# Output projection of the last segment: its first 384 columns under the last attention unit's combination

## The chip, the cores and the metric

The kernel runs on one core of a Trainium2 chip. TensorE (PE) does the matrix products, VectorE (DVE) and ScalarE (ACT) the element-wise work and all reading of PSUM, GpSimd (POOL) element-wise work in SBUF; SyncE (SP), ACT and POOL also issue DMA transfers. The metric is the device time of one execution in microseconds. Every engine takes its instructions in the order in which the program lists them and waits at each for the semaphores that it names.

## The reference

One transformer block on a 2048 x 576 input, float32:

```python
mod = (_silu(c) @ w_mod).reshape(c.shape[0], 6, 1, -1)
sa, ca, ga, sb, cb, gb = (mod[:, 0], ..., mod[:, 5])
h = _layernorm(x) * (1 + ca) + sa
x = x + ga * _A_ref(h, wq, wk, wv, wo, beta)     # attention
h = _layernorm(x) * (1 + cb) + sb
return x + gb * _B_ref(h, w_gate, w_up, w_down)  # (silu(h @ w_gate) * (h @ w_up)) @ w_down
```

The attention has 32 heads of 18 columns and works on 4 segments of 512 rows. In each segment it mixes causal softmax attention within the segment with a linear attention over a memory of the segments before it, and multiplies the 576 columns by `wo`. The FFN has 4608 inner columns.

## The kernel before

Every float32 product is made of three products of float32r parts: an operand x is split into `hi`, a cast of it, and `lo = x - hi`, and hi\*hi, hi\*lo and lo\*hi are summed in PSUM.

The program has three stages. The first makes q, k, v of the segments. The second runs 32 units (segment s, group q of 4 heads, u = 8 s + q). The third is the FFN, in 18 pairs of blocks of 256 inner columns, done by a scheme with seven products instead of eight (`step`, `prod`).

The second stage's order is written out by hand: `ORDER` (L60 to L94) has one line of tokens for each unit, and `act` turns each token into the instructions of one small step. What matters here: `a` makes a unit's scores in banks of the tags `s1` (3 buffers) and `s2` (3 buffers); `V0123` makes P\*V of a unit into a bank `av` of the tag `x` (2 buffers); `E` copies it to SBUF (`avs`, ACT, L726); `c` transposes it (`px`, PE, L735); `d` divides by the row sums and adds the result into the unit's 72 columns of `o` (DVE, L743 to L752). `>` moves a token to the next unit; `y` and a number are steps that make inputs of the FFN, `M0` to `M3` and `X` a half of an output projection.

The output projection of segment s takes `o` (4 groups i of 128 rows, 576 columns) through these steps: `wo_r` transposes columns 0 to 511 of a group into one bank `pto` (four transposes, L789); `wo_s` casts it to `hh` (ACT, L795); `wo_t` makes `hl` from `pto` and `hh` (DVE, L799); `wo_z` and `wo_z2` do the same with columns 512 to 575 of all four groups (`ptr`, `or`; L772, L778, L779); `wo_m` makes 14 products for each group and half h of the 576 output columns into a bank `pw` (L815): for segment 3 first the eight with `hh`, then four with `hl`, then two with `or`; `wo_x` adds `pw` to the input rows `xr` (DVE, L820), and after h = 1 a DMA stores them (L822).

For segments 0 to 2 these steps stand among later units. Segment 3 has no later units: its steps are written out behind `ORDER`, after the pools of the second stage are closed, with a PSUM pool of their own (`pst`, tags `x` with 4 and `w` with 2 buffers). In between stand, on the SP queue, the loads of the FFN's first weights (`O`, L1290: pair 0's two halves) and of four of its inputs (`y`, L1277 and L1278), and within the loop over the eight (i, h) the first weights are prepared: `sum_o` (L1312) makes sums of weight blocks, `prep_w` casts (`wh`, ACT, L1321) and subtracts (`wl`, DVE, L1322), `y_here` makes three more inputs (L1197, L1199), `store_o` writes the sums to DRAM for later (`oD`, L1296), `store_r` does so with the cast row remainders (`rD`, L1315). `O` has two buffers, so that the next pair's load (L1290) into a buffer waits for the store of `oD` that reads it.

Of the kernel before, what the change touches and what calls it, by code (L numbers as in the profile page):

```python
# [7 lines left out]
F32 = mybir.dt.float32  # L8
# [3 lines left out]
ALU = mybir.AluOpType  # L12
PSUM = bass.MemoryType.PSUM
DRAM = bass.MemoryType.DRAM

P = 128
S = 2048
# [5 lines left out]
L = 512  # L23
# [29 lines left out]
WC = 4  # L53
# [40 lines left out]
)  # L94
LNA = 1
# [1 line left out]
S1B, S2B, XB = 3, 3, 2  # L97
# [8 lines left out]
def block(ctx: ExitStack, tc: tile.TileContext, x, wqk, wv, wo, beta, wgu, wd, c, w_mod, wm01, out):  # L106
    nc = tc.nc
    def pool(stk, name, bufs=1, **kw):
        return stk.enter_context(tc.tile_pool(name=name, bufs=bufs, reuse_waits="tile", **kw))
# [16 lines left out]
    ident = cst.tile([P, P], F32, tag="ident", name="ident")  # L126
# [159 lines left out]
    p2, p2q, p2r, p7 = ExitStack(), ExitStack(), ExitStack(), ExitStack()  # L286
# [43 lines left out]
    with ExitStack() as p1:  # L330
        raw = pool(p1, "raw1", 2)
        x1 = pool(p1, "x1")
        w1 = pool(p1, "w1")
        wk = pool(p1, "wk1", 2)
        ps = pool(p1, "ps1", 2, space=PSUM)
# [84 lines left out]
        with ExitStack() as p0:  # L420
# [39 lines left out]
            for b in range(3):  # L460
                n = P if b < 2 else 64
# [202 lines left out]
    vp = pool(p2, "vp", 2)  # L664
    pp_ = pool(p2, "pp")
    wk = pool(p2, "wk2", 2)
    ps = pool(p2, "ps2", 2, space=PSUM)

    def load_unit(u):
        if u < NU:  # L670
            load_stack(u, u % NB)
# [82 lines left out]
    ot, vq = {}, {}  # L754

    def load_v(s, j):
        if j == 0:
            vq[s] = vp.tile([P, 4, VC], F32, tag="vq", name=f"vq{s}")
        nc.sync.dma_start(vq[s][:, j, :], vD[s][:, j, :])
# [7 lines left out]
    oT, orr, pto = {}, {}, {}  # L767

    def wo_z(s):
        pt = ps.tile([P, 4, P], F32, tag="x", name="ptr", bufs=XB if s < 3 else 4)  # L770
        for i in range(4):
            nc.tensor.transpose(pt[:64, i, :], ot[s][:, i, 512:576], ident)  # L772
        pto[s] = pt
# [7 lines left out]
    def load_xr(s, i):  # L781
        xr = o3.tile([P, D], F32, tag="xr", name="xr") if s < 3 or i in (0, 3) else xp.tile([P, D], F32, tag="xs", name="xr")
        nc.sync.dma_start(xr, x[s][:, i, :])
        return xr

    def wo_r(s, i):
        pt = ps.tile([P, 4, P], F32, tag="x", name="pto", bufs=XB if s < 3 else 4)
        for kt in range(4):
            nc.tensor.transpose(pt[:, kt, :], ot[s][:, i, 128 * kt:128 * kt + 128], ident)  # L789
        pto[s, i] = pt  # L790
        oh, ol = [hvp.tile([P, L], F32R, tag=f"{n}{i % 2}", name=n).rearrange("p (a b) -> p a b", b=P) for n in ("hh", "hl")]
        oT[s, i] = (oh, ol, load_xr(s, i) if s < 3 else xr3[i])

    def wo_s(s, i):
        nc.scalar.copy(oT[s, i][0], pto[s, i])  # L795

    def wo_t(s, i):
        oh, ol, _ = oT[s, i]
# [2 lines left out]
    wps = {}  # L801

    def wo_m(s, i, h, c):
        oh, ol, _ = oT[s, i]
        sl = slice(288 * h, 288 * h + 288)
        if c == 0:
            wps[0] = ps.tile([P, L], F32, tag="x" if s < 3 else "w", name="pw", bufs=XB if s < 3 else 2)
        ops = []
        for k in range(4):
            ops += [(oh[:, k], woh[:, k, sl]), (oh[:, k], wol[:, k, sl]), (ol[:, k], woh[:, k, sl])]  # L810
        if s == 3:
            ops = [ops[n] for n in (0, 1, 3, 4, 6, 7, 9, 10, 2, 5, 8, 11)]
        ops += [(orr[s][:, i], woh[:, 4, sl]), (orr[s][:, i], wol[:, 4, sl])]
        for n in range(14 * c // WC, 14 * (c + 1) // WC):
            nc.tensor.matmul(wps[0][:, :288], lhsT=ops[n][0], rhs=ops[n][1], start=(n == 0), stop=(n == 13))  # L815

    def wo_x(s, i, h):
        xr = oT[s, i][2]
        sl = slice(288 * h, 288 * h + 288)
        nc.vector.tensor_tensor(xr[:, sl], wps[0][:, :288], xr[:, sl], op=ALU.add)  # L820
        if h == 1:
            (nc.scalar if (s, i) == (2, 3) else nc.sync).dma_start(xD[s][:, i, :], xr)  # L822

# [536 lines left out]
    T, SG, AC, AP = {}, {}, {}, {}  # L1360
# [158 lines left out]
    with tc.manual_schedule():  # L1519
# [7 lines left out]
        def step_a(u):  # L1527
            if u not in flows:
                ma, mb = [], []
                flows[u] = (chain(*[p2_step(u, j, ma) for j in range(4)]), p1_seq(u + 2, mb), ma, mb)  # L1530
            scores(*flows[u])

        def act(tok, u):
            nonlocal w3, o3, opl_, woh, wol
            if tok[0] in "<>":
                act(tok[1:], u + (1 if tok[0] == ">" else -1))
            elif tok == "a":
                step_a(u)
            elif tok == "U":
                load_unit(u + 3)  # L1540
            elif tok[0] == "v":
                load_v(u // 8 + 1, int(tok[1]))
            elif tok == "SA":
                stage_a()
            elif tok == "SB":
                stage_b()
            elif tok[0] == "y":
                parts[int(tok[1:])]()
            elif tok == "O":
                p2q.close()  # L1550
                w3 = pool(p2r, "w3", side="right")
                o3 = pool(p2r, "o3", 2, side="right")
                opl_ = pool(p2, "op2", side="right")
                woh = w3.tile([P, 5, D], F32R, tag="woh", name="woh")
                wol = w3.tile([P, 5, D], F32R, tag="wol", name="wol")
                ot[0] = opl_.tile([P, 4, D], F32, tag="o0", name="o0")
            else:
                event(tok, u)
# [3 lines left out]
                act(tok, u)  # L1562
        p2.close()
        mid.close()
        ps = pool(p2r, "pst", 2, space=PSUM)
        xp = pool(p4, "xp", 2)
        yp = pool(p4, "yp")
        y = yp.tile([P, 7, 5, L], F32R, tag="y", name="y")
# [4 lines left out]
        xr3 = {i: load_xr(3, i) for i in range(3)}  # L1573
# [9 lines left out]
        xr3[3] = load_xr(3, 3)  # L1583
        load_y(0, 5)
        load_y(0, 3)
        wo_r(3, 0)
        wo_z(3)
        wo_r(3, 1)
        wo_s(3, 0)
        wo_t(3, 0)  # L1590
        wo_z2(3)
        wo_s(3, 1)
        wo_t(3, 1)
        gw = iter(MP[:PF])
        for i in range(4):
            for h in range(2):
                for c in range(WC):
                    n = 8 * i + 4 * h + c
# [28 lines left out]
        ps = pool(p4, "ps4", 1, space=PSUM)  # L1627
# [6 lines left out]
        n, nw = 0, PF  # L1634
# [200 lines left out]
```

## Time and profile before

| | us |
|---|---|
| runs, median of 3 | 1833.85 (1831.41 to 1834.4) |
| profiled execution, its own time | 1828.63 |
| span of the profiled execution | 1826.8 |
| mean granted TensorE clock in it | 0.999 of full |
| the 512 products on L815, segments 0 to 3: first and last start | 310.1, 563.5 |
| first product of the FFN (L1357) | 563.60 |

The runs are of the kernel alone; the profiled execution is one more, and its span is what lies between the first and the last event of its trace. In a row of the order of time stand the start, the time from the start of the first to the end of the last instruction of the row, the engine, the line, the operation, what it writes and reads, and in brackets the idle time of the engine before it with what ended it. In a row of windows stand the window, its length, the busy time of PE, of PE's weight loads, DVE, ACT and POOL with the number of instructions, the granted clock, the busy share of the DMA engines and GB/s. In a row of the waits of the SP queue stand the waiting line, what it waited for, the sum, the number of waits and the longest one.

### The profile page before, as it was taken

How to read it: one execution, taken by the hardware profiler on the slowest of the kernel's cores; microseconds unless marked ns; L12 is line 12 of the kernel's file. 1: busy time of each engine (PE TensorE's matmuls, PEld its weight loads, DVE VectorE, ACT ScalarE, POOL GpSimd, SP SyncE). 2: the span in 40 equal slices, each digit the busy share in tenths (PEclk: the TensorE clock that was granted, in tenths of full speed). 3: DMA queues.
4: the chain of work that ended last, by engine and by line, in shares of the span. 5: the costliest groups of instructions: out<-in, count | busy, mean ns of one | idle time of the engine just before them, and what ended most of it. 6: DMA issues, size and time to landing. Idle time of an engine off the chain costs nothing.

```text
span 1826.8 us, 31122 instructions
## 1 busy us (share of the span) xinstructions
PE 1802.9 (99%) x11061; PEld 1514.3 (83%) x11061; DVE 1490.4 (82%) x3309; ACT 953.8 (52%) x2137; POOL 492.6 (27%) x702
## 2 busy tenths in 40 slices
PE   8999999999999999999999999999999999999999
PEld 5888766766668888888888888888888888888888
DVE  7566588998968888888888898668888888888886
ACT  6443577777875444544454444434544544544541
POOL 2000146555660554465354544100000000000000
PEclk9999999999999999999999999999999999999999
DMA  8677765567659545544653454594334324323331
GB/s 297 227 237 274 242 179 162 150 197 208 186 175 315 175 163 182 191 154 164 200 173 128 151 170 133 168 303 151 96 96 128 101 85 129 107 79 129 106 103 52
DMA packets 178562, 304.49 MB, mean 167 GB/s; under 512 B 25304, under 2 KB 108184, under 8 KB 176616
## 3 DMA queue, kind: packets, MB, share of 16 engines
q1 hardware_dynamic: 151032, 248.66, 43.0%
q10 hardware_dynamic: 27376, 53.86, 8.4%
q8 instruction: 87, 1.43, 0.3%
q14 instruction: 67, 0.55, 0.1%
HBM read 188.42 MB, written 113.33 MB: 165 GB/s over the span
## 4 chain that ended last, share of the span: by engine, by line
PE 92%; DMA 3%; DVE 3%; issue 1%; ACT 1%; SPq 0%; ACTq 0%; DVEq 0%
PE A L1357 24%; PE pd L1485 13%; PE C L1357 12%; PE pd L1466 10%; PE B L1357 6%; PE pp L553 4%; PE av L714 4%; PE pw L815 3%; PE s L691 3%; PE s L204 3%; PE pv L582 2%; PE pp L839 2%; DMA y<-yD 1%; DMA qs<-mr 1%; PE pw L892 1%; PE pn L951 1%
## 5 line engine op out<-in xcount | busy, mean ns | idle before, releaser
L1357 PE MATMUL A<-y,wh 128*128 128x512 f32 x1152 | 406.1, 393 | 1.3 <-ACT B L1403 0.9
L1357 PEld LDWEIGHTS A<-y,wh 128*128 128x128 f32 x1152 | 216.6, 188 | 46.0 <-ACT B L1403 2.2
L1322 DVE TENSOR_TENSOR wl<-O,wh 128x256 fp32r<-128x256 f32 x504 | 249.4, 500 | 2.1 <-ACT wh L1321 1.6
L219 DVE CUSTOM_DVE_ANT_0 junk<-s,tri 128x384 bf16<-128x384 f32 (+3 forms) x512 | 221.6, 486 | 30.0 <-PE s L204 13.2
L1357 PE MATMUL A<-y,wl 128*128 128x512 f32 x576 | 226.8, 394 | 0.0
L1471 DVE TENSOR_TENSOR acc<-acc,pd 128x576 f32<-128x576 f32 x216 | 162.2, 752 | 58.9 <-PE pd L1466 51.2
L1357 PE MATMUL C<-y,wh 128*128 128x512 f32 x576 | 203.0, 393 | 0.5 <-DVE cu L1380 0.5
L1321 ACT CAST wh<-O 128x256 fp32r<-128x256 f32 x504 | 197.5, 405 | 0.7 <-DMA yD<-st 0.7
L697 ACT ACTIVATE Pt<-s 128x512 f32<-128x512 f32 (+2 forms) x384 | 179.4, 528 | 31.6 <-PE s L691 18.1
L1485 PE MATMUL pd<-dh,ah 128*128 128x288 f32 x640 | 189.1, 295 | 0.5 <-DVE x L1489 0.5
L1495 DVE TENSOR_TENSOR acc<-acc,pd 128x576 f32<-128x576 f32 x156 | 116.9, 750 | 89.1 <-PE pd L1485 88.3
L1485 PE MATMUL pd<-dh,al 128*128 128x288 f32 x640 | 189.1, 295 | 0.0
L1312 POOL TENSOR_TENSOR O<-O 128x384 f32<-128x384 f32 x132 | 150.4, 1153 | 143.3 <-DMA O<-in_wgu_dram 55.5
L1485 PE MATMUL pd<-dl,ah 128*128 128x288 f32 x640 | 188.8, 295 | 0.0
L1426 ACT CAST ah<-sg 128x512 fp32r<-128x512 f32 x192 | 119.1, 620 | 78.4 <-DVE sg L1381 71.9
L1427 DVE TENSOR_TENSOR al<-sg,ah 128x512 fp32r<-128x512 f32 x192 | 136.2, 709 | 10.3 <-ACT ah L1426 10.2
L1466 PE MATMUL pd<-dh,ah 128*128 128x288 f32 x448 | 133.0, 297 | 0.0
L1466 PE MATMUL pd<-dh,al 128*128 128x288 f32 x448 | 132.5, 296 | 0.0
L1466 PE MATMUL pd<-dl,ah 128*128 128x288 f32 x448 | 132.3, 295 | 0.0
L1485 PEld LDWEIGHTS pd<-dh,ah 128*128 128x128 f32 x640 | 120.8, 189 | 6.8 <-DVE x L1489 0.8
L1485 PEld LDWEIGHTS pd<-dl,ah 128*128 128x128 f32 x640 | 120.5, 188 | 7.1
L1357 PEld LDWEIGHTS C<-y,wh 128*128 128x128 f32 x576 | 108.3, 188 | 21.5 <-DVE cu L1380 1.3
(410 smaller groups left out, 4337.7 us busy)
## 6 DMA issues: line engine op xcount, KB each, us to landing
O<-in_wgu_dram SPq DMA_DIRECT2D x36, 768.0 KB
O<-oD SPq DMA_DIRECT2D x36, 512.0 KB
oD<-O ACTq DMA_DIRECT2D x34, 512.0 KB
ks<-kD SPq DMA_DIRECT2D x64, 216.0 KB
qs<-qD SPq DMA_DIRECT2D x64, 216.0 KB
O<-in_wgu_dram SPq DMA_DIRECT2D x36, 384.0 KB
rD<-wr ACTq DMA_DIRECT2D x36, 336.0 KB
wr<-rD SPq DMA_DIRECT2D x35, 336.0 KB
```

The costliest lines, as they stand in the source:

```text
L219: nc.vector.tensor_tensor_reduce(junk[:, :n], bank[:, n * o:n * o + n], tri[:, L - n:], 1.0, -3e38, op0=ALU.add, op1=ALU.max, accum_out=mx ...
L697: nc.scalar.activation(pt[:, hs[0]:hs[-1] + 1:2, :n], bank[:, :n * per].rearrange("p (a b) -> p a b", a=per), AF.Exp, scale=SCALE)
L1312: eng.tensor_tensor(o[:, d], o[:, a], o[:, b], op=op)
L1321: nc.scalar.copy(wh, o)
L1322: later.append(lambda: nc.vector.tensor_tensor(wl, o, f32(wh), op=ALU.subtract))
L1357: nc.tensor.matmul(bank, lhsT=a, rhs=b, start=(first and n == 0), stop=(n == 6), skip_group_check=not first)
L1426: nc.scalar.copy(ah, src)
L1427: later.append(lambda: nc.vector.tensor_tensor(al, src, f32(ah), op=ALU.subtract))
L1466: nc.tensor.matmul(pd[:, i, :288], lhsT=a[:, tk], rhs=w, start=(k == 0), stop=(k == 2))
L1471: nc.vector.tensor_tensor(o, o, pd[:, :, :288], op=ALU.add)
L1485: nc.tensor.matmul(pd[:, i, :288], lhsT=a[:, tk], rhs=w, start=(k == 0), stop=(k == 5))
L1495: nc.vector.tensor_tensor(o, o, pd[:, :, :288], op=ALU.add)
```

## The change

In the last line of `ORDER`, tokens are put in around the last unit's `c` and `d`. `t0` and `t1` transpose columns 0 to 383 of the groups 0 and 1 of segment 3, `s0` and `s1` cast them, and `w0` and `w1` make the first six products (k = 0 to 2, with `hh`) of group 0 for both halves. Behind `ORDER` only what depends on columns 384 to 511 is left of these steps (`wo_k3`, a cast of 128 columns, products from the seventh on); `wo_t` still makes `hl` of all 512 columns at once. The pool `pst` is gone: the second stage's PSUM pool stays open until the projection is done, `pto` uses the banks of tag `s1`, `pw` those of `s2`, and `ptr` those of `x`.

```diff
-    "... >M2 >M3 y130 >X >V0123 >E y126 >c >d y131",
+    "... >M2 >M3 y130 >X >V0123 >E t0 t1 s0 y126 >c w0 w1 s1 >d y131",
...
-    ps = pool(p2, "ps2", 2, space=PSUM)
+    ps = pool(p2r, "ps2", 2, space=PSUM)
...
-        pt = ps.tile([P, 4, P], F32, tag="x", name="ptr", bufs=XB if s < 3 else 4)
+        pt = ps.tile([P, 4, P], F32, tag="x", name="ptr", bufs=XB)
...
-    def wo_r(s, i):
-        pt = ps.tile([P, 4, P], F32, tag="x", name="pto", bufs=XB if s < 3 else 4)
-        for kt in range(4):
+    def wo_r(s, i, early=False):
+        if s < 3:
+            pt = ps.tile([P, 4, P], F32, tag="x", name="pto", bufs=XB)
+        else:
+            pt = ps.tile([P, 4, P], F32, tag="s1", name="pto", bufs=S1B)
+        for kt in range(3 if early else 4):
             nc.tensor.transpose(pt[:, kt, :], ot[s][:, i, 128 * kt:128 * kt + 128], ident)
...
+    def wo_k3(i):
+        nc.tensor.transpose(pto[3, i][:, 3, :], ot[3][:, i, 384:512], ident)
+
+    def wo_s(s, i, k=slice(0, 4)):
+        nc.scalar.copy(oT[s, i][0][:, k], pto[s, i][:, k])
...
-        if c == 0:
-            wps[0] = ps.tile([P, L], F32, tag="x" if s < 3 else "w", name="pw", bufs=XB if s < 3 else 2)
+        if s < 3 and c == 0:
+            wps[0] = ps.tile([P, L], F32, tag="x", name="pw", bufs=XB)
+        elif s == 3 and (i, h) not in wps:
+            wps[i, h] = ps.tile([P, L], F32, tag="s2", name="pw", bufs=S2B)
...
-        for n in range(14 * c // WC, 14 * (c + 1) // WC):
-            nc.tensor.matmul(wps[0][:, :288], lhsT=ops[n][0], rhs=ops[n][1], start=(n == 0), stop=(n == 13))
+        n0 = 6 if s == 3 and i == 0 else 0
+        for n in range(6) if c < 0 else range(n0 + (14 - n0) * c // WC, n0 + (14 - n0) * (c + 1) // WC):
+            nc.tensor.matmul(pw[:, :288], lhsT=ops[n][0], rhs=ops[n][1], start=(n == 0), stop=(n == 13))
...
+            elif tok in ("t0", "t1"):
+                wo_r(3, int(tok[1]), True)
+            elif tok in ("s0", "s1"):
+                wo_s(3, int(tok[1]), slice(0, 3))
+            elif tok in ("w0", "w1"):
+                wo_m(3, 0, int(tok[1]), -1)
...
-        ps = pool(p2r, "pst", 2, space=PSUM)
...
-        wo_r(3, 0)
+        wo_k3(0)
         wo_z(3)
-        wo_r(3, 1)
-        wo_s(3, 0)
+        wo_k3(1)
+        wo_s(3, 0, slice(3, 4))
         wo_t(3, 0)
         wo_z2(3)
-        wo_s(3, 1)
+        wo_s(3, 1, slice(3, 4))
         wo_t(3, 1)
```

On PE, before, behind the last unit's P\*V (`av`), to the first products with `hl` (`o_6638` is segment 3's `o`):

```order
L714 MATMUL av<-Pt,vq_6127 32x128 x2
L735 MATMUL px<-ident,avs 128x128 [waits DVE_49,Activation_49]
L735 MATMUL px<-ident,avs 128x128 x3
L789 MATMUL pto<-ident,o_6638 128x128 [waits DVE_49,PE_49]
L789 MATMUL pto<-ident,o_6638 128x128 x2
L789 MATMUL pto<-ident,o_6638 128x128 [waits DVE_49,Pool_49]
L772 MATMUL ptr<-ident,o_6638 64x128 x4
L789 MATMUL pto<-ident,o_6638 128x128 x4
L815 MATMUL pw<-woh,hh 128x288 [waits Activation_49]
```

The same place with the change (of the products only those that wait are shown):

```order
L714 MATMUL av<-Pt,vq_6127 32x128 x2
L792 MATMUL pto<-ident,o_6638 128x128 x6
L735 MATMUL px<-ident,avs 128x128 [waits DVE_49,Activation_49]
L735 MATMUL px<-ident,avs 128x128 x3
L826 MATMUL pw<-woh,hh 128x288 [waits Activation_49]
...
L798 MATMUL pto<-ident,o_6638 128x128 [waits DVE_49,Pool_49]
L772 MATMUL ptr<-ident,o_6638 64x128 [waits PE_49]
L772 MATMUL ptr<-ident,o_6638 64x128 x3
L798 MATMUL pto<-ident,o_6638 128x128 [waits Activation_49]
L826 MATMUL pw<-woh,hh 128x288 [waits Activation_49]
...
L826 MATMUL pw<-woh,hl 128x288 [waits DVE_49]
...
L826 MATMUL pw<-woh,or 128x288 [waits DVE_49]
```

Six of the eight transposes stand ahead of `px` and wait for nothing; twelve products stand between `px` and the transpose of columns 384 to 511, which is the one that still waits for DVE's add into `o`. The same stretch on ACT, before:

```order
L726 COPY avs<-av 128x512 [waits PE_49,Activation_49]
L795 CAST hh<-pto 128x512 [waits PE_49]
L778 CAST or<-ptr 64x512 [waits PE_49]
L795 CAST hh<-pto 128x512 [waits PE_49,Activation_49]
```

and with the change:

```order
L726 COPY avs<-av 128x512 [waits PE_49,Activation_49]
L801 CAST hh<-pto 128x384 [waits PE_49]
L801 CAST hh<-pto 128x384 [waits PE_49,Activation_49]
L801 CAST hh<-pto 128x128 [waits PE_49]
L778 CAST or<-ptr 64x512 [waits PE_49]
L801 CAST hh<-pto 128x128 [waits PE_49]
```

Each cast of `hh` is split in two, and the first parts stand right behind `avs`. On DVE, POOL and SP the instructions and their order are the same.

More of the change, by code (lines that the diff above doesn't have):

```diff
@@ L791, in wo_r @@
         oh, ol = [hvp.tile([P, L], F32R, tag=f"{n}{i % 2}", name=n).rearrange("p (a b) -> p a b", b=P) for n in ("hh", "hl")]
-        oT[s, i] = (oh, ol, load_xr(s, i) if s < 3 else xr3[i])
-    def wo_s(s, i):
-        nc.scalar.copy(oT[s, i][0], pto[s, i])
+        oT[s, i] = (oh, ol, load_xr(s, i) if s < 3 else None)
+    def wo_k3(i):
+        nc.tensor.transpose(pto[3, i][:, 3, :], ot[3][:, i, 384:512], ident)
+    def wo_s(s, i, k=slice(0, 4)):
+        nc.scalar.copy(oT[s, i][0][:, k], pto[s, i][:, k])
     def wo_t(s, i):
@@ L805, in wo_m @@
         sl = slice(288 * h, 288 * h + 288)
-        if c == 0:
-            wps[0] = ps.tile([P, L], F32, tag="x" if s < 3 else "w", name="pw", bufs=XB if s < 3 else 2)
+        if s < 3 and c == 0:
+            wps[0] = ps.tile([P, L], F32, tag="x", name="pw", bufs=XB)
+        elif s == 3 and (i, h) not in wps:
+            wps[i, h] = ps.tile([P, L], F32, tag="s2", name="pw", bufs=S2B)
+        pw = wps[0] if s < 3 else wps[i, h]
         ops = []
@@ L812, in wo_m @@
             ops = [ops[n] for n in (0, 1, 3, 4, 6, 7, 9, 10, 2, 5, 8, 11)]
-        ops += [(orr[s][:, i], woh[:, 4, sl]), (orr[s][:, i], wol[:, 4, sl])]
-        for n in range(14 * c // WC, 14 * (c + 1) // WC):
-            nc.tensor.matmul(wps[0][:, :288], lhsT=ops[n][0], rhs=ops[n][1], start=(n == 0), stop=(n == 13))
+        if c == WC - 1:
+            ops += [(orr[s][:, i], woh[:, 4, sl]), (orr[s][:, i], wol[:, 4, sl])]
+        n0 = 6 if s == 3 and i == 0 else 0
+        for n in range(6) if c < 0 else range(n0 + (14 - n0) * c // WC, n0 + (14 - n0) * (c + 1) // WC):
+            nc.tensor.matmul(pw[:, :288], lhsT=ops[n][0], rhs=ops[n][1], start=(n == 0), stop=(n == 13))
     def wo_x(s, i, h):
-        xr = oT[s, i][2]
+        xr = oT[s, i][2] if s < 3 else xr3[i]
+        pw = wps[0] if s < 3 else wps.pop((i, h))
         sl = slice(288 * h, 288 * h + 288)
-        nc.vector.tensor_tensor(xr[:, sl], wps[0][:, :288], xr[:, sl], op=ALU.add)
+        nc.vector.tensor_tensor(xr[:, sl], pw[:, :288], xr[:, sl], op=ALU.add)
         if h == 1:
```

2 rows, old and new, of the table ORDER are left out of this document.

## The prediction

> **What bounds the kernel now.** I read the page first, then the order of time around the place of the change, engine by engine, then the clock, and at last the DMA queue behind it.
>
> ```profile
> span 1826.8 us, 31122 instructions
> PE 1802.9 (99%) x11061; PEld 1514.3 (83%) x11061; DVE 1490.4 (82%) x3309; ACT 953.8 (52%) x2137; POOL 492.6 (27%) x702
> PE 92%; DMA 3%; DVE 3%; issue 1%; ACT 1%; SPq 0%; ACTq 0%; DVEq 0%
> ```
>
> TensorE is busy 99% of the span and makes 92% of the chain of waits: what shortens the kernel is a hole in PE, or a stretch in which PE runs below its rate. Both lie where the last attention unit hands over to the output projection of segment 3. PE in order of time there:
>
> ```profile
> 540.22 0.62 PE L714 MATMUL av<-Pt,vq 128*32 128x256 f32 x12
> 541.60 0.66 PE L735 MATMUL px<-ident,avs 128*128 128x128 f32 x4 [0.76 <-ACT avs L726]
> 544.13 0.52 PE L789 MATMUL pto<-ident,o 128*128 128x128 f32 x3 [1.88 <-DVE tmp L751]
> 545.16 0.30 PE L789 MATMUL pto<-ident,o 128*128 128x128 f32 x1 [0.51 <-DVE o L752]
> 545.30 0.61 PE L772 MATMUL ptr<-ident,o 128*64 128x128 f32 x4
> 545.74 1.02 PE L789 MATMUL pto<-ident,o 128*128 128x128 f32 x4
> 546.41 0.59 PE L815 MATMUL pw<-woh,hh 128*128 128x288 f32 x1
> ...
> 549.60 0.29 PE L815 MATMUL pw<-woh,hh 128*128 128x288 f32 x1
> ...
> 551.47 0.60 PE L789 MATMUL pto<-ident,o 128*128 128x128 f32 x4
> ```
>
> The brackets are holes: 0.76, 1.88 and 0.51 us. The first 14 products take 549.60 - 546.41 = 3.19 us, the next 14 only 551.47 - 549.60 = 1.87 us (0.134 us each). The granted clock (the third number from the right in these windows) says why:
>
> ```profile
> 545.60:545.80 0.20, 0.20 (x4) 0.20 (x3) 0.00 (x0) 0.20 (x1) 0.00 (x0) 0.91 1.11 451
> ...
> 549.00:549.20 0.20, 0.20 (x3) 0.20 (x3) 0.00 (x0) 0.00 (x0) 0.20 (x1) 0.56 1.62 379
> ```
>
> It falls to half inside the first window and comes back inside the second, 3.4 us later; the 3.19 us hold 1.32 us of that. What the holes wait for is on ScalarE and VectorE:
>
> ```profile
> 540.96 0.58 ACT L726 COPY avs<-av 128x512 f32<-128x512 f32 x1 [3.13 <-PE av L714]
> 545.50 0.59 ACT L795 CAST hh<-pto 128x512 fp32r<-128x512 f32 x1 [3.95 <-PE pto L789]
> ```
>
> ```profile
> 544.02 0.99 DVE L752 TENSOR_TENSOR o<-o,tmp 128x288 f32<-128x288 f32 x1
> 546.12 0.69 DVE L799 TENSOR_TENSOR hl<-pto,hh 128x512 fp32r<-128x512 f32 x1 [1.10 <-ACT hh L795]
> ```
>
> The last unit's columns are added into o until 545.01. Everything of segment 3's projection stands behind that add, though 384 of 576 columns were ready before.
>
> **The change part by part.** *Six transposes ahead of px.* Their inputs are older and their banks idle, so they start when av has issued, about 540.6. At 0.66 / 4 = 0.165 us each at most they take 0.99 us and end by 541.6, where px waits for avs anyway. Cost 0; at worst 0.2 us on the chain over DVE.
>
> *Two casts of 128x384 on ACT.* They follow avs (541.54), each at most the 0.59 us of a 128x512; the first is there at about 542.1, the second at 542.7. ACT has nothing else until 545.50. Cost 0.
>
> *Twelve products after px.* They start with the first cast, and after px (541.60 + 0.66 = 542.26), and take 12 x 0.134 = 1.6 us: 542.3 to 543.9. The transposes that wait for the add start at 545.16 as before. Even at half rate (12 x 0.27 = 3.2 us) they end at 545.5, 0.3 us late. Cost 0, cover 1.3 us.
>
> *What is left behind the add.* One transpose at 545.16, four ptr to 545.74, one more transpose. ACT casts 128 columns instead of 512; no row has that form, and it lies between nothing and 0.59 us; I take 0.3, near half. So hh is there at 545.8, not 546.09, and the first product starts at 545.85. hl follows on DVE at 545.82 + 0.69 = 546.51, then the or tile, whose ACT cast still ends near 546.56, by about 547.25. PE: two products to 546.12; a new wait of 0.4; four with hl from 546.53 to 547.06; a new wait of 0.2; two with or to 547.55; eight of the second half to 548.62. The transposes that stood at 551.47 stand at 548.62: **PE gains 2.85 us**, 0.56 by the earlier start and 2.29 by 16 products in 2.77 us for 28 in 5.06. This supposes full clock. If the clock still halves from 545.8 to 549.2, the same steps end near 549.7 and the gain is 1.8; below that no row points.
>
> The Trainium skill (TensorE: Matmul & The Clock Gate, Part 1, the HAM clock gate, and Part 4, PE-mode transpose) says that an idle window of about 3.4 us halves the clock and that transposes don't count as busy. By that rule the clock stays full here, since the longest stretch without a product shrinks from 540.84-546.41 to 543.9-545.85, and the sum is 2.85; by the row of before it is 1.8. The trace of before agrees with the rule: half clock for 3.4 us behind a stretch of transposes alone.
>
> *Does the rest follow?* The windows show PE without a hole from 549 to 570 (its busy time is the second number), so the projection and the first products of the FFN move up rigidly, with ACT, DVE and the DMAs that these release. What doesn't move is the work of the DMA engines (the second number from the right is their busy share):
>
> ```profile
> 549.00:564.00 15.00, 15.00 (x113) 14.86 (x113) 12.60 (x25) 8.02 (x17) 2.93 (x3) 0.99 1.03 353
> 564.00:570.00 6.00, 6.00 (x27) 4.91 (x27) 5.55 (x12) 4.35 (x11) 0.00 (x0) 1.00 1.04 351
> ...
> 583.00:594.00 11.00, 10.19 (x42) 7.40 (x41) 10.82 (x22) 5.75 (x14) 0.00 (x0) 1.00 0.97 330
> ```
>
> ```profile
> 600.00:700.00 100.00, 100.00 (x547) 87.73 (x546) 85.67 (x141) 47.65 (x106) 52.16 (x52) 1.00 0.50 169
> ```
>
> They are full before 570 at 351 GB/s. In 583-594 DVE is the bound (10.82 of 11 us, PE 10.19), and from 600 on PE again. So the shift must pass DVE at 583, and that needs a load:
>
> ```profile
> 564.69 0.88 SPq L1329 DMA_DIRECT2D dr__8971<-in_wd_dram  x2
> 567.56 0.33 SPq L1290 DMA_DIRECT2D O<-in_wgu_dram  x1
> 567.94 0.60 SPq L1296 DMA_DIRECT2D oD<-O  x1
> 576.71 0.33 SPq L1290 DMA_DIRECT2D O<-in_wgu_dram  x1
> ```
>
> ```profile
> SPq L1290 <- DMA oD<-O: 6.5, 1, 6.5
> SPq L1290 <- DVE wl L1322: 1.6, 1, 1.6
> ```
>
> ```profile
> L1296 SPq EVENT_SEMAPHORE  x1: 17/17/17, 582.6 to 582.6; - x1
> ```
>
> ```profile
> 575.90 0.41 ACT L1321 CAST wh<-O 128x256 fp32r<-128x256 f32 x1
> ```
>
> ```profile
> 575.93 0.76 DVE L1322 TENSOR_TENSOR wl<-O,wh 128x256 fp32r<-128x256 f32 x2
> ...
> 582.88 0.55 DVE L1312 TENSOR_TENSOR O<-O 128x384 f32<-128x384 f32 x1
> ```
>
> ```profile
> 586.82 0.50 PE L1357 MATMUL C<-y,wh 128*128 128x512 f32 x1 [0.48 <-DVE cu L1380]
> ```
>
> The load at 576.71 (pair 1's second half of gate and up weights) overwrites a buffer that the store of 567.94 reads. SP waited 6.5 us for that store, to 568.54 + 6.5 = 575.06, then 1.6 us for the wl that ends at 576.69. It landed at 582.6 (SP's next instruction waits for it), 5.9 us after its issue, and DVE's sum used it at 582.88: slack 0.28 us. After the change wl is done by 573.85, but the store still needs its bytes through full engines: I keep 575.06, issue 575.1, landing 581.0. DVE is there at 582.88 - 2.85 = 580.03 and waits 0.97 us. What passes is 582.88 - 581.0 = **1.9 us**; PE's wait at 586.82 grows by the rest. Bounds: 2.85 if the store moves too, 0.28 if load and landing don't move at all. ACT's wh at 575.90 needs the load of 567.56 in the same way; with the same 5.9 us from its old issue that one lands near 573.5, against a wish for 573.05: a stall of at most 0.4 us, which the 0.97 covers.
>
> One more transfer is near: the last of the FFN's four inputs.
>
> ```profile
> 556.27 0.59 ACTq L1296 DMA_DIRECT2D oD<-O  x1
> ...
> 568.70 0.33 ACTq L1315 DMA_DIRECT2D rD<-wr  x1
> ...
> 575.15 0.31 ACTq L1315 DMA_DIRECT2D rD<-wr  x1
> ```
>
> ```profile
> 568.43 0.40 PE L1357 MATMUL C<-y,wh 128*128 128x512 f32 x1
> ```
>
> ```profile
> oD<-O ACTq DMA_DIRECT2D x34, 512.0 KB
> ...
> rD<-wr ACTq DMA_DIRECT2D x36, 336.0 KB
> ```
>
> C needs it at 565.58 instead of 568.43. The second of the two loads at 564.69 takes its queue slot and wasn't held up, so it had landed by 565.2. ACT's store of 556.27 now starts at 553.4 and may go ahead of it, at most 512 KB / 351 GB/s = 1.5 us: a stall of 0 to 1.1 us, which the 0.97 us at 581 mostly hides.
>
> The sum against the profiled execution (1828.63 us, of which 1826.8 is the span): span 1824.9, execution 1826.7. The runs' median is 1833.85, so **1832.0 us**.
>
> **Rivals.** *A: all of it passes.* The store of 567.94 waited behind a load that was itself held 1.9 us, by the store of 556.27:
>
> ```profile
> SPq L1290 <- DMA oD<-O: 1.9, 1, 1.9
> ```
>
> Both now start earlier; against it stands the share of 1.04. 2.85 us: 1831.0.
>
> *B: the queue takes it back.* If the load of 576.71 lands at 582.6 again (it shares the engines with more neighbours), only the slack of 0.28 is left: 1833.6. For it: the full share before; against: SP was held by DVE, not by a DMA, in the last 1.6 us.
>
> *C, slower: ACT's stores overtake SP's.* The two rD stores are issued at 568.70 and 575.15, behind the SP store of 567.94 or when it has landed; at 565.85 and 572.3 both stand ahead of or beside it. Each is 336 KB / 351 GB/s = 1.0 us. With both ahead the SP store lands at 575.06 + 2.0 = 577.1, and the load issued there lands at 583.0 at the earliest, 0.1 us after DVE's old 582.88, and up to 1.0 us later still if the second rD store runs beside the load as well: 0.6 us slower in the middle, 1834.4. It decides from the point at which more than 1.9 us of ACT's bytes are put ahead. The Trainium skill (Trainium Kernel Development and Optimization, Key Constraints) says that DMAs from the SP, ACT and POOL queues run on the same 16 engines and interleave, which speaks for this rival; no row here shows the order in which single packets went.
>
> *D: it doesn't do what it says*, the clock halves all the same. PE gains 1.8, DVE meets the landing at 581.0 without a wait: 1832.1, hardly to be told from the forecast in the time.
>
> **How the numbers follow.** Forecast 0.32 and D 0.10, together 0.42 at 1832.0; A 0.25; B 0.18; C 0.15. The three runs of before span 3.0 us and the profiled one lies 5.2 under their median, so a median may move by 1.5 either way. The likeliest case alone: 1830.5 to 1833.5. With A and C and their scatter: 1828.8 to 1835.2. A measurement of this kernel can tell about 0.2%, 3.7 us, from no change. Faster by more than that (under 1830.2) needs A with a low median, or a bit more hidden than I count: 0.25 x 0.35 and 0.42 x 0.2, with a little of B, 0.19. Slower by more than 3.7 us needs C repeated at a later pair, or scatter on B and C: 0.07. Within: 0.74.
>
> **What would show it.** Right: twelve products between px and the add; px still near 541.6; no half clock (if the mean granted clock isn't 1.00, D); the transposes of the third group near 548.6; PE idle near 586 longer by about 1 us, with the second O load issued near 575.1 and landed near 581. A shows as that load before 574, B as its landing at 582.6, C as later. It would be wrong altogether if px came later than 541.8, or if the C products waited more than 2 us for an input of the FFN.

## The result and the profile after

| | before | with the change |
|---|---|---|
| median of 22 runs each (us) | 1832.07 | 1834.91 |
| profiled execution: span (us) | 1826.8 | 1832.7 |
| mean granted TensorE clock in it | 0.999 | 0.998 |

The ratio is 1.002 with a 95% interval of 1.0012 to 1.0029: the kernel became about 0.2% slower, some 3 us, where 1832.0 us and a gain of 1.9 us were forecast. The time lies inside the wide range given (1828.8 to 1835.2), by luck: the forecast was counted from a median of three runs, 1833.85, and 22 runs of the kernel before have 1832.07. From 1833.85 the same loss of 2.84 us would have ended at 1836.69, outside. The sign is the wrong one.

Two profiled executions can't be laid on each other by their times from the start, since they differ before the change begins: the last unit's add into `o` (L752) starts at 544.02 us before and at 546.20 after.

```profile
546.20 0.99 DVE L752 TENSOR_TENSOR o<-o,tmp 128x288 f32<-128x288 f32 x1
```

So every time below that compares two kernels is a **shift**: the distance of an instruction from this add, less the same distance in the kernel before. The FFN's 6792 products are the same in all kernels and in the same order, so each has its counterpart. A negative shift is a gain.

The order of time of PE, after:

```profile
542.91 0.87 PE L792 MATMUL pto<-ident,o 128*128 128x128 f32 x6
543.74 0.66 PE L735 MATMUL px<-ident,avs 128*128 128x128 f32 x4
...
545.70 0.29 PE L826 MATMUL pw<-wol,hh 128*128 128x288 f32 x1
547.34 0.30 PE L798 MATMUL pto<-ident,o 128*128 128x128 f32 x1 [1.35 <-DVE o L752]
...
548.72 0.79 PE L826 MATMUL pw<-woh,hl 128*128 128x288 f32 x4 [0.19 <-DVE hl L805]
...
550.90 0.60 PE L792 MATMUL pto<-ident,o 128*128 128x128 f32 x4
...
562.91 0.40 PE L1369 MATMUL A<-y,wh 128*128 128x512 f32 x1
```

This is the gain as forecast (how much of it is the state of the clock is said further down). The FFN's first product stands 562.91 - 546.20 = 16.71 us behind the add, before 563.60 - 544.02 = 19.58: a shift of -2.87 us. The loss comes later, on PE at three places:

```profile
568.52 0.50 PE L1369 MATMUL C<-y,wh 128*128 128x512 f32 x1 [0.62 <-DMA y<-yD]
```

```profile
581.62 0.50 PE L1369 MATMUL A<-y,wh 128*128 128x512 f32 x1 [1.33 <-ACT tb L1398]
591.82 0.50 PE L1369 MATMUL C<-y,wh 128*128 128x512 f32 x1 [3.48 <-DVE cu L1392]
```

The product at 591.82 is the one that stood at 586.82 before: 45.62 us behind the add instead of 42.80, a shift of +2.82. Behind that hole the granted clock (third number from the right in the windows) is at half:

```profile
592.00:593.00 1.00, 1.00 (x5) 0.82 (x6) 1.00 (x3) 0.47 (x1) 0.00 (x0) 0.93 1.09 392
593.00:596.00 3.00, 3.00 (x9) 2.12 (x8) 3.00 (x7) 2.17 (x6) 0.00 (x0) 0.50 0.91 314
```

DVE was late because it waited twice for a load of O (pair 1's two halves), and these were late because SP's queue stood:

```profile
580.16 1.15 DVE L1324 TENSOR_TENSOR O<-O 128x384 f32<-128x384 f32 x2 [1.88 <-DMA O<-in_wgu_dram]
...
587.88 1.15 DVE L1324 TENSOR_TENSOR O<-O 128x384 f32<-128x384 f32 x2 [2.56 <-DMA O<-in_wgu_dram]
```

```profile
SPq L834 <- DMA oD<-O: 10.4, 1, 10.4
SPq L1302 <- DMA oD<-O: 8.7, 1, 8.7
```

```profile
558.93 0.32 SPq L834 DMA_DIRECT2D xD<-xr  x1
```

```profile
569.70 1.44 SPq L834 DMA_DIRECT2D xD<-xr  x3
571.23 1.15 SPq L1341 DMA_DIRECT2D dr__8969<-in_wd_dram  x2
572.48 0.45 SPq L1302 DMA_DIRECT2D O<-in_wgu_dram  x1
572.98 0.60 SPq L1308 DMA_DIRECT2D oD<-O  x1
582.39 0.33 SPq L1302 DMA_DIRECT2D O<-in_wgu_dram  x1
```

Before, the four stores of `xD` went out from 556.29 to 564.60. Now SP stands 10.4 us ahead of the second one, until a store `oD<-O` has landed, and everything behind it in the queue (wd rows, O, oD, O) is late: the two loads of O leave 26.28 and 36.19 us behind the add, before 23.54 and 32.69. The store is ACT's:

```profile
555.71 0.59 ACTq L1308 DMA_DIRECT2D oD<-O  x1
```

SP's `xD` store neither reads nor writes what that store does. What ties them is in the program as it is built: each DMA raises one of eight completion semaphores when it has landed, they are given out in turn over both queues in the order of the program's list, and a DMA's issuer first waits until the semaphore's previous DMA has landed. Here are the entries around the place (place in the list of DMAs, queue, transfer; the count that it waits for on each semaphore HW0 to HW7; the semaphore that it raises):

```
before   498 ACT oD<-O   waits HW1:62           raises HW1 to 63
         503 SP  xD<-xr  waits HW6:62           raises HW6
         504 SP  xD<-xr  waits HW7:62           raises HW7
         506 ACT rD<-wr  waits HW1:63           raises HW1
change   496 ACT oD<-O   waits HW7:61           raises HW7 to 62
         503 SP  xD<-xr  waits HW7:61, HW6:62   raises HW6
         504 SP  xD<-xr  waits HW7:62           raises HW7
         505 ACT rD<-wr  waits HW0:63           raises HW0
```

In both sources ACT's store stands at the same step of the loop (n = 24 of 32). In the list of the built program the change moved it two places up, ahead of a load of `y` and one of `xr`; by what rule the build orders the list is not shown here. In the kernel before the next user of its semaphore was a store of ACT itself. Now it is SP's second `xD` store.

### The profile page after: what moved, and what is told of

It reads as the page before. It is cut to its first block, busy times and chain, and to the rows that moved or that the text cites. A ratio compares the mean times of both kernels' runs of the same rounds, so it can differ in the third digit from the quotient of the medians.

```text
span 1832.7 us, 31122 instructions
## 1 busy us (share of the span) xinstructions
PE 1805.2 (98%) x11061; PEld 1514.0 (83%) x11061; DVE 1490.3 (81%) x3309; ACT 954.6 (52%) x2139; POOL 494.2 (27%) x702
## 4 chain that ended last, share of the span: by engine, by line
PE 89%; DMA 6%; DVE 3%; issue 1%; ACT 1%; SPq 0%; POOL 0%; ACTq 0%; DVEq 0%
PE A L1369 24%; PE pd L1497 13%; PE C L1369 12%; PE pd L1478 10%; PE B L1369 6%; PE pp L553 4%; PE av L714 4%; PE s L691 3%; PE s L204 3%; PE pv L582 2%; PE pw L826 2%; DMA y<-yD 2%; PE pp L851 2%; DMA qs<-mr 1%; PE pn L963 1%
## 5 line engine op out<-in xcount | busy, mean ns | idle before, releaser
L1439 DVE TENSOR_TENSOR al<-sg,ah 128x512 fp32r<-128x512 f32 x192 | 136.0, 709 | 10.4 <-ACT ah L1438 10.3
```

The source lines that it names most:

```text
L1439: later.append(lambda: nc.vector.tensor_tensor(al, src, f32(ah), op=ALU.subtract))
```

## The experiments

The theories: **T1**, the shared semaphore holds SP's queue, and that is the loss. Its rival **T2**: the DMA engines are full, and the semaphore is only the place at which SP happens to stand. For what was left of the loss: **T3**, PE's gain is lost where DVE waits, in order, for pair 1's second load of O, which did not move up; its rival **T4**, it is lost in DVE's own work. The table has the shift of the FFN's products at three times of the kernel before, and the runs against that kernel, taken beside them on the same chip.

| kernel | shift at 563.5 | 582 | 660 | median | ratio, 95% interval |
|---|---|---|---|---|---|
| the change | -2.87 | -0.18 | +3.37 | 1834.91 | 1.002 (1.0012 to 1.0029) |
| change, store at n = 25 | -2.86 | -1.82 | -0.06 | 1833.39 | 0.9998 (0.9985 to 1.001) |
| before, store at n = 23 | -1.25 | +0.84 | +4.65 | 1834.99 | 1.0012 (1.0001 to 1.0022) |
| before, store at n = 25 | +0.89 | +0.89 | +1.69 | 1834.35 | 1.0008 (0.9996 to 1.0021) |
| change, store at n = 23 | -2.84 | -0.61 | +3.74 | 1835.37 | 1.0014 (1.0004 to 1.0025) |
| n = 25, SP's oD first | -2.84 | -2.84 | -2.23 | 1831.81 | 0.9999 (0.9989 to 1.0008) |
| n = 25, sums later | -1.54 | -1.54 | -0.92 | 1831.34 | 0.999 (0.9976 to 1.0005) |
| before, sums later | +0.73 | +0.73 | +1.23 | 1833.43 | 1.0011 (0.9999 to 1.0023) |
| change (n = 24), sums later | -2.85 | -1.07 | +0.16 | 1831.61 | 0.9996 (0.9986 to 1.0007) |
| n = 25, both | -2.85 | -2.14 | -1.54 | 1831.55 | 0.9991 (0.9976 to 1.0006) |
| n = 24, both | -2.85 | +3.59 | +2.48 | 1835.87 | 1.0022 (1.0012 to 1.0032) |
| before, both | +0.01 | +0.02 | +0.58 | 1834.03 | 1.0007 (0.9997 to 1.0017) |
| n = 25, both, six products more | -3.64 | -3.64 | -3.27 | 1829.48 | 0.9992 (0.9981 to 1.0002) |

The kernel before had medians of 1832.31 beside the first four variants, 1831.85 beside the next four, 1832.15 beside the last four.

**The store's place in the list.** The edit, here in the changed kernel (the others differ in the number, and in the kernel that it is made in):

```diff
                     if n == 24:
                         nc.scalar.activation(omg[:, 0:1], omg[:, 0:1], AF.Silu)
+                    if n == 25:
                         store_o(0, 0)
```

> The changed kernel with ACT's first store of oD listed one step of the loop later (n = 25 instead of 24, some 0.5 us of products); the Silu table step stays at n = 24. Theory T1: the loss comes from a shared completion semaphore. Each DMA takes one of eight in turn, in the order of the program's list, and its issuer first waits for the DMA that had it before; in the changed kernel SP's second xD store has the one of ACT's oD store, and SP stood 10.4 us. Here that store takes another one, whose next user is an ACT store. So SP's xD stores follow their sums without a hole over 2 us for a DMA of ACT, pair 1's loads of O come about 2.8 us earlier than in the kernel before, and the time is 1.9 to 2.9 us under the kernel before (ratio 0.9984 to 0.9990). Theory T2: the loss comes from the full DMA engines, which ACT's and SP's stores share; the semaphore is only where SP waits. Then 0.5 us of delay change nothing: 2 to 4 us above the kernel before (ratio 1.001 to 1.002), and SP stands as long at the next place.

> The kernel before with the same store listed one step earlier (n = 23): it now shares its semaphore with SP's second xD store, as in the changed kernel. T1: SP's second xD store is issued only when ACT's oD store has landed, near 567.5 on the time line of the kernel before; pair 1's second load of O lands 3 us later, DVE's slack for it is 0.28 us, so the kernel is 2.5 to 5 us slower (ratio 1.0014 to 1.0027) without anything of the change in it. T2: a store 0.5 us earlier onto engines that are full anyway: same time within 1 us.

> The kernel before with the same store one step later (n = 25): it shares its semaphore with SP's fourth xD store. T1: only that store and what is behind it in SP's queue wait, until about 568, against 564 before; pair 1's loads of O are 1 to 3 us late: 0.5 to 3.5 us slower (ratio 1.0003 to 1.002), less than with n = 23. T2: same time within 1 us.

> Control: the changed kernel with the store one step earlier (n = 23). It shares the same semaphore with the same xD store as in the changed kernel. T1 and T2 alike: SP stands about 10 us before its second xD store and the time is that of the changed kernel, 2 to 4 us above the kernel before (ratio 1.001 to 1.002).

With n = 25 SP's four `xD` stores follow one another again (the changed kernel, n = 25):

```profile
560.28 5.82 SPq L834 DMA_DIRECT2D xD<-xr  x4
566.72 3.19 SPq L1341 DMA_DIRECT2D dr__8969<-in_wd_dram  x2
570.97 0.33 SPq L1302 DMA_DIRECT2D O<-in_wgu_dram  x1
571.35 0.60 SPq L1308 DMA_DIRECT2D oD<-O  x1
579.77 0.33 SPq L1302 DMA_DIRECT2D O<-in_wgu_dram  x1
```

The shift at 660 falls from +3.37 to -0.06, and the run with n = 23 (same semaphore as with the change) stays at +3.74. In the runs the ratio falls from 1.002 (1.0012 to 1.0029) to 0.9998 (0.9985 to 1.001), and the intervals don't meet. The store itself hardly moved:

```profile
556.63 0.61 ACTq L1308 DMA_DIRECT2D oD<-O  x1
```

It leaves ACT's queue 556.63 - 547.11 = 9.52 us behind the add (which starts at 547.11 here), with n = 24 555.71 - 546.20 = 9.51. So a store that comes earlier or later is not what makes the difference. In the kernel before, without anything of the change, n = 23 makes SP stand too:

```profile
SPq L822 <- DMA oD<-O: 10.7, 1, 10.7
```

It loses 5.9 us of shift from 563.5 to 660, and its ratio is 1.0012 (1.0001 to 1.0022). With n = 25 there, SP waits 5.3 us for ACT's store ahead of its fourth `xD` store; the trace loses 0.8 us from 582 to 660, as T1 expects, but the interval of the runs holds 1. T1 stands. T2 had expected no effect in the kernel before. But T1 had also expected 1.9 to 2.9 us of gain with n = 25, and the trace shows none at 660. The gain is there until 582 and then goes: the second load of O leaves 579.77 - 547.11 = 32.66 us behind the add, before 576.71 - 544.02 = 32.69. It did not move, and DVE and PE run into it (n = 25, DVE and PE):

```profile
585.42 1.15 DVE L1324 TENSOR_TENSOR O<-O 128x384 f32<-128x384 f32 x2 [1.18 <-DMA O<-in_wgu_dram]
```

```profile
589.36 0.50 PE L1369 MATMUL C<-y,wh 128*128 128x512 f32 x1 [1.75 <-DVE cu L1392]
```

Both loads of O wait for a store that reads their buffer (n = 25):

```profile
SPq L1302 <- DMA oD<-O: 8.7, 2, 7.8
```

The first load waits for ACT's store and leaves 570.97 - 547.11 = 23.86 us behind the add, before 23.54: the store left 2.7 us earlier than in the kernel before (9.52 us behind the add against 12.25) and brought the load nothing. Behind that load SP's own `oD` is issued, 24.24 us behind the add against 23.92, and for this one the second load waits 7.8 us. For the part of the loss that is left that fits T2, with the DMA engines full from 556 to 572 (busy shares of 1.02 to 1.05); no run here changes their load alone.

**The load, and who waits for it.** One edit lists SP's store of `oD`, for which that load waits, ahead of pair 1's first load of O; the other lists the sums over pair 1's second half, needed only in pair 1, one step later on DVE:

```diff
-                        if dl and k == 3:
+                        if dl and k == 1:
                             store_o(0, 1, nc.sync)
```

```diff
-                        if dl and 9 <= k < 13:
+                        if dl and k in (9, 10, 12, 13):
                             for j in (0, 1):
-                                sum_o(nx, (k - 9) // 2, 2 * ((k - 9) % 2) + j, nc.vector)
+                                sum_o(nx, k // 12, 2 * ((k - k // 12) % 2 == 0) + j, nc.vector)
```

> The kernel with the store one step later (n = 25), and SP's store of oD (pair 0, second half) listed ahead of pair 1's first load of O instead of behind it. With n = 25 alone the gain of 1.8 to 2.3 us, counted from the last add into o, held until 580 on the time line of the kernel before and was gone at 585: DVE waited 1.18 us for pair 1's second load of O, which had not moved (issued 32.66 us behind the add, 32.69 in the kernel before), and PE 1.75 us behind it. Theory T3: that load is late because the store that it waits for stands behind 7 us of other bytes in full DMA engines. Here the store is issued about 4 us earlier, so the load goes out 1.5 to 3 us earlier, DVE waits under 0.4 us for it, and the time is 1 to 2.5 us under the kernel before (ratio 0.9986 to 0.9995), unless the first load, now behind the store's 512 KB, takes up to 1.5 us of it back. Theory T4: the gain ends in DVE's own work between 583 and 594, where it has hardly a pause: then the time is that of n = 25 alone, within 1 us of the kernel before.

> The kernel with the store one step later (n = 25), and the two steps of sums over pair 1's second half of O on DVE listed one step of the FFN later (k = 12 and 13 instead of 11 and 12). These sums are needed only in pair 1. T3: the load itself is not urgent; it costs because DVE, in order, waits for it ahead of the combination (cu) for which PE waits. With the sums later DVE does not wait there, cu starts 1.2 to 2.3 us earlier, PE's hole near 587 is under 0.5 us, the clock stays full: 1.5 to 2.8 us under the kernel before (ratio 0.9985 to 0.9992). T4: DVE has as much work as before and cu is as late: within 1 us of the kernel before.

> Control: the kernel before with the sums listed one step later, nothing else. T3: in the kernel before DVE met that load without a wait (0.28 us of slack), so only PE's hole of 0.48 us near 586.8 can go: the same time, at most 0.6 us faster (ratio 0.9997 to 1.0000). T4: the same time too. So what the run before this gains over the kernel before is not the sums' place alone.

> The changed kernel as it was given (store at n = 24, semaphore shared with SP's second xD store) with the sums one step later. T1: SP still stands 9 to 10.5 us before its second xD store; pair 1's first load of O is still late, DVE still waits some 1.9 us for it near 580 and PE 1.3 us behind; the second wait is smaller. So 0 to 2.5 us above the kernel before and at least 1.5 us above the kernel with n = 25 and the same sums (ratio 1.000 to 1.0014). If only the half-rate clock behind the second hole had cost the time, it would be as fast as that one.

With the store first, the second load leaves at 577.81 (the last 0.33 us of the row of loads), 577.81 - 547.96 = 29.85 us behind the add and 2.8 us earlier than with n = 25 alone. DVE meets it with a wait of 0.22 us, and the shift stays near its full size, -2.84 at 582 and -2.23 at 660:

```profile
570.92 7.22 SPq L1302 DMA_DIRECT2D O<-in_wgu_dram  x2
```

```profile
584.29 1.15 DVE L1324 TENSOR_TENSOR O<-O 128x384 f32<-128x384 f32 x2 [0.22 <-DMA O<-in_wgu_dram]
```

With the sums later DVE doesn't wait there at all. That kernel's execution had the clock at half in the projection, which is why it starts from -1.54; of this it keeps -0.92. So T3 holds in the traces, and T4 falls: the same DVE work lets the gain through. The runs say less: 0.9999 (0.9989 to 1.0008) and 0.999 (0.9976 to 1.0005) lie beside 1. In medians that is 0.04 and 0.5 us under the kernel before, where at least 1 and 1.5 us were expected.

Two more expectations missed. The control with the sums alone did not get up to 0.6 us faster: from 582 to 660 it loses 0.5 us, so the later sums cost that much elsewhere. And n = 24 with the later sums was not 1.5 us above n = 25 in the runs (1831.61 and 1831.34). In its trace SP stands 9.8 us, and from 563.5 to 660 it loses 3.01 us where n = 25 with the later sums loses 0.62; the runs don't confirm it. So with the later sums alone a held queue costs nothing that the runs show.

**Both, with the one place of the store as the only difference.**

> The changed kernel with ACT's store one step later (n = 25), SP's store of oD ahead of pair 1's first load of O, and the sums over pair 1's second half one step later. Apart, the second and the third left 2.2 and 0.9 us of PE's gain at 660 us of the kernel before, against nothing with n = 25 alone. T3 (the gain was lost where DVE waits, in order, for pair 1's second load of O): nothing in the FFN's first 60 us waits for a load any more, 2.2 to 2.9 us are kept at 660, and the time is 1.5 to 2.9 us under the kernel before (ratio 0.9984 to 0.9992). T4 (the gain ends in DVE's own work): no better than with either alone, within 1 us of the kernel before.

> The kernel of the run before this with the store where the change had it (n = 24), so that SP's second xD store waits for ACT's store again; nothing else differs. T1: SP stands 9 to 10.5 us, pair 1's loads and the first wd rows are 3 to 5 us late, the first waits for them near 578 to 582 stay: 1 to 3 us slower than the run before this (ratio to the kernel before 0.9993 to 1.0010). T2 (the semaphore is only the place where SP waits): the same time as the run before this.

> Control: the kernel before with SP's store of oD ahead and the sums later, without the change in the output projection. T3: there was only 0.5 us of PE waiting there to win, so 0 to 0.8 us faster (ratio 0.9996 to 1.0000), and the change itself is worth 1.5 to 2.5 us between this run and the one with n = 25 and both. T4: those two steps are what gains, and this run is as fast as that one.

With both edits, n = 25 and n = 24 give 0.9991 (0.9976 to 1.0006) and 1.0022 (1.0012 to 1.0032). The intervals don't meet: one place of one store in the list is worth 4.3 us of the medians here, 1 to 3 having been expected, and 4.02 us of shift at 660. It is more than with the sums later alone, since with SP's store of `oD` ahead 512 KB more stand in the held queue in front of pair 1's first load, and DVE needs that load first: it leaves 26.94 us behind the add, with the sums later alone 25.68. In the kernel with n = 24 SP stands again, and DVE and PE behind it:

```profile
SPq L834 <- DMA oD<-O: 10.6, 1, 10.6
```

```profile
581.34 1.15 DVE L1324 TENSOR_TENSOR O<-O 128x384 f32<-128x384 f32 x2 [3.46 <-DMA O<-in_wgu_dram]
```

```profile
582.80 0.80 PE L1369 MATMUL A<-y,wh 128*128 128x512 f32 x1 [3.84 <-ACT tb L1398]
```

In the kernel before the two edits bring nothing (+0.58 at 660; 1.0007, 0.9997 to 1.0017, where up to 0.8 us of gain was expected), so in the traces it is the change that gains between that run and n = 25 with both: 0.58 + 1.54 = 2.1 us of shift. The medians differ by 2.5 us, but the two intervals overlap. That n = 25 with both keeps 1.54 and not the 2.2 to 2.9 us expected (in medians 0.6 us under the kernel before, and not 1.5 to 2.9) has two parts: 0.7 us at the first C products, before 582, and the 0.6 us of the later sums.

**A version with more of the projection early.** In the 1.35 us that PE waits for the add there is room for six more products, those of group 1, half 0 (`w2`, behind `s1`):

```diff
-    "... >c w0 w1 s1 >d y131",
+    "... >c w0 w1 s1 w2 >d y131",
...
-            elif tok in ("w0", "w1"):
-                wo_m(3, 0, int(tok[1]), -1)
+            elif tok in ("w0", "w1", "w2"):
+                wo_m(3, int(tok[1]) // 2, int(tok[1]) % 2, -1)
...
-        n0 = 6 if s == 3 and i == 0 else 0
+        n0 = 6 if s == 3 and 2 * i + h < 3 else 0
```

> The kernel with n = 25 and both steps, and six more products of the projection early: those of group 1, half 0, behind the second early cast, in the 1.36 us that PE still waits for the last add into o. Six products take 6 x 0.134 = 0.8 us out of the work behind the add. T3: 0.8 us faster than the run with n = 25 and both, if the loads still come in time: 2.3 to 3.6 us under the kernel before (ratio 0.9980 to 0.9988). T4, or the full DMA engines as the bound again: the same time as that run.

```profile
547.32 0.30 PE L798 MATMUL pto<-ident,o 128*128 128x128 f32 x1 [0.58 <-DVE o L752]
```

The hole shrinks from 1.36 to 0.58 us and the shift grows from -2.85 to -3.64, by the 0.8 us expected; -3.27 is left at 660. Its median, 1829.48, is the lowest of all, 2.7 us under the kernel before and 4.6 under the kernel before with both edits, run beside it. Against the kernel before the interval (0.9981 to 1.0002) still touches 1, so that a gain over it is likely and not shown.

## Why the prediction was wrong, point by point

*Six transposes and two casts at no cost*: right. px starts at 543.74, as soon as the copy `avs` is done. *Twelve products under the cover of the add*: right, they end 1.35 us before the transpose that waits for it; 1.3 was forecast.

*What is left behind the add*: right in the sum. Of the two new waits of PE, forecast at 0.4 and 0.2 us, one of 0.19 is there. The cast of 128 columns was a guess of 0.3 us:

```profile
547.68 0.27 ACT L801 CAST hh<-pto 128x128 fp32r<-128x128 f32 x1 [3.23 <-PE pto L798]
```

The third group's transposes come 550.90 - 546.20 = 4.70 us behind the add; 4.60 was forecast. **PE gains 2.85 us**: measured 2.87 at the FFN's first product, and 2.84 to 2.86 in six of the seven variants that have the change's twelve early products as they were given. That it fits so well hangs on the execution of the kernel before, which had one stretch at half clock in the projection. Beside the one that had none (n = 23, at -1.25) the same trace gains 2.87 - 1.25 = 1.62 us, and beside those with a stretch twice as long up to 3.8.

*The clock (rival D)*: it stayed full there in seven of these eight kernels, and halved in the one with n = 25 and the sums later (1.54 us of gain; 1.8 was forecast):

```profile
549.00:550.00 1.00, 0.80 (x4) 0.57 (x4) 0.94 (x2) 1.00 (x3) 0.00 (x0) 0.85 1.02 424
550.00:552.00 2.00, 2.00 (x11) 2.00 (x10) 1.67 (x4) 0.70 (x2) 1.12 (x2) 0.50 0.99 402
```

So "by that rule the clock stays full here" was too firm: it is likelier to, and not more. The same rule was read as borne out by the trace of before, but one of five projections without the change kept the full clock behind the same stretch of transposes.

*"The projection and the first products of the FFN move up rigidly, with ACT, DVE and the DMAs that these release"*: **this is the step that failed.** I let each DMA go when its data were ready and its queue had come to it, and took stores on ACT's queue to bear on SP's only through the shared bandwidth, "at most 512 KB / 351 GB/s = 1.5 us". A DMA also waits for the last one that had its completion semaphore, on whichever queue that was, and the change gave ACT's 512 KB store a new successor. It was issued at 555.71, and the SP queue went on at 569.70: 14.0 us, some nine times the 1.5. Undone (n = 25), 3.4 us of shift come back. The built program's list of waits shows the tie before any run, and I read it for PE and ACT and not for SP: that SP's instructions and their order are the same was true and not enough.

*What passes: 1.9 us*. Mis-sized as well, even without the held queue. I had the second load of O issued at 575.1, since the store of 567.94 would land as before and only DVE's last read would be earlier. With n = 25 it was issued 32.66 us behind the add, which is 576.68 on the time line of the kernel before, so nothing moved. SP's waits for that store were 6.5 us before and 7.8 with n = 25: it landed 571.35 + 0.60 + 7.8 - 547.11 = 32.64 us behind the add, where the forecast kept 575.06 - 544.02 = 31.04. That DVE's last read was earlier brought nothing. This is rival B, whose 0.28 us of gain stands against 0.55 measured at 586 and nothing from 660 on. What none of the cases had was the second cost of it: behind the hole that the load leaves on PE (1.75 us) the clock is at half for 3.41 us.

*Stall of C by the last `y`: 0 to 1.1 us*: right in size, 0.62 us of wait; of the nine kernels with early products four have it, with 0.41 to 0.78 us, and five don't. It is not hidden: with n = 25 and both edits, where no load is late afterwards, the 0.7 us lost there stay lost until 582. *Rival C* had the right direction, by another mechanism and in another place: ACT's `rD` stores ahead of an SP store, 0.6 us. What the change pays is 5.7 us of shift between 563.5 and 586 (-2.87 to +2.82).

Still open: at the turn to the FFN's second pass, near 1210, PE waits 0.3 to 2.7 us for an input `y` in single executions, and between 1200 and 1250 the traces lose from 0.1 to 3.9 us, the most with n = 25. The three traces that lose over 3 us there (n = 25; before with the sums later; n = 24 with the sums later) have waits of 2.69, 2.00 and 2.02 us and a stretch at half clock right behind them, the others waits up to 1.93 and none. Whether that depends on the kernel or on the execution was not tried; it may be part of why the runs show less than the shifts at 660.

## What to carry to other kernels

When a change shifts a DMA in the program's list, by even two places, read again for every queue which DMA each one waits for: a completion semaphore that is given out in turn ties an in-order queue to a slow transfer of another one. A gain of a few us on the bounding engine passes only as far as the loads behind it move too, so follow the first load with little slack back to what releases it, and look for a non-urgent reader that stands ahead of urgent work on an in-order engine. Compare single traces by an anchor inside them, since they drift apart by more than the effect: the add started between 544.02 and 549.59 us in the fourteen traces.

## What the runs showed of the hardware that was not expected

**A half-rate stretch has a fixed length and a fixed grid.** In the clock records of all fourteen traces each stretch at half rate, but for the cut one at the end, lasts 3.41 or 6.83 us, and their starts within a trace lie whole multiples of 3.4133 us apart: 143.36 us in the changed kernel (42 times), 266.24 and 177.49 us in the kernel before with n = 23 (78 and 52 times). A hole of 1.75 us on PE (n = 25, at 589.36) was followed by one, and so was the hole of 1.36 us in the variant with later sums, while the other kernels' holes of 1.35 to 1.37 us at that place were not. The Trainium skill (TensorE: Matmul & The Clock Gate, Part 1, what's actually happening) says that the clock's activity window is 3413 ns long and free-running, and the starts agree with that. It gives one idle window of about 3.4 us as what halves the clock; here the half rate also came behind shorter holes, and not each time. So the projection of the kernel before is itself a draw: it was at half rate once 3.41 us (two traces), 6.83 us (two) or not at all (one), which spreads the shift at 563.5 from +0.89 to -1.25.

**Two queues with work shared the engines by packets, not by bytes.** ACT's store of 555.71 moved nothing before 560 us, and then this (the changed kernel, 562 to 564 and 564 to 566 us: packets, MB, share of 16 engines; q1 is SP's queue, q10 ACT's):

```profile
q1 hardware_dynamic: 108, 0.62, 83.5%
q10 hardware_dynamic: 108, 0.11, 17.8%
```

```profile
q1 hardware_dynamic: 167, 0.60, 77.2%
q10 hardware_dynamic: 168, 0.17, 25.0%
```

The packets are one to one, but ACT's are of 1 KB (0.11 MB / 108) and SP's of 3.6 to 5.7 KB, so the store gets 18 to 25% of the engines' time. That is how its 512 KB came to take some 9 of the 14.0 us; in the more than 4 us ahead of that nothing of it moved, and why is open. The Trainium skill (DMA: Bandwidth & Descriptors, Queues, rings and completion order) says that an engine takes turns between queues at the granularity of packets; these counts agree.
